# Infini-attention and a gated feed-forward layer: an order planned with margins, a second buffer for phi of Q, and a changed start

## The chip, the cores and the metric

The program runs on one core of one Trainium2 chip. The metric is the time of one execution on the device in microseconds. The kernel before took 832.03 us as the median of three runs (831.11 to 833.02).

Five engines work side by side: TensorE (PE; its weight loads are listed as PEld), VectorE (DVE), ScalarE (ACT), GpSimd (POOL), and SyncE (SP), which issues the DMAs. Each runs its own instructions strictly in the order in which the program lists them and waits on semaphores for the others.

## The reference

A layer with 2,048 tokens, width 512 and 32 heads of 16; the tokens fall in four segments of 512.

```python
x = A_x
h = x + attention(layernorm(x))        # N = 4 segments, H = 32 heads
h2 = h + geglu(layernorm(h))           # 512 -> 1376 -> 512

# attention, segment s, every head
logits = qs @ ks.T * scale + causal_mask
a_dot = softmax(logits) @ vs
pq = phi(qs)                           # phi(t) = t + 1 if t > 0 else exp(t)
a_mem = (pq @ M) / (pq @ z + 1e-6)     # memory of the earlier segments
o = sigmoid(beta) * a_mem + (1 - sigmoid(beta)) * a_dot
M, z = M + phi(ks).T @ vs, z + phi(ks).sum(0)

# feed-forward
out = (gelu(hn @ w_gate) * (hn @ w_up)) @ w_down
```

All data is float32. The kernel gets near that accuracy from TensorE's faster rounded format by splitting an operand into a high part (rounded) and a low part (the rest) and summing three products: high by high, high by low and low by high (`SPLIT`).

## The kernel before, in words

**Work.** The attention is cut into 16 units, one for each pair of a chunk of eight heads and a segment (`UNITS`, index `U`), and each unit into two halves of four heads (index `Q`, 0 to 31). Before them `ln1(s)` normalises the rows of segment `s`, transposes them on TensorE and splits them into `XT`. For each unit `qkv(U)` projects Q and K (`project`, L619), splits the result into `hl` (L680 on ScalarE, L682 on VectorE), sends it by DMA to the layouts `stq` and `stk`, computes phi of Q and K (`phi`: Relu L627 and Exp L629 on ScalarE, L631 on VectorE), and adds to the memory. `vproj` (L648) projects V for two units at a time.

Two passes over the scores follow for each half. `pass_a(Q)` computes scores with queries on the partitions (L797) and takes each row's extreme value on VectorE (L807, 512 instructions), which is moved into a free row of `stq`. `pass_b(Q)` computes the scores again with keys on the partitions (L862, L869), now with the extreme value subtracted by the matmul itself, takes the exponential on ScalarE (L876), masks the diagonal blocks on GpSimd (L879), and accumulates with V (L900) into one bank, `pv`. `mem(U)` reads phi of Q twice: for the denominator (L756) and, after a trip of the reciprocal through memory, for the numerator (L772).

`wo_seg` applies the output projection (L973); `ln2` normalises again; `ffn` computes gate and up products (L1145) and `down` the last product (L1206), with VectorE adding the result to the sum (L1211).

**Order.** No loop nest sets the order. Each piece of work is entered in a planner (`Sched`) as an operation of one engine with a planned duration, its operands and a due time. `Sched.run` walks through a planned time: among the operations that could start within a window of 0.059 us of the earliest one, it takes the one with the smallest due time, and emits it. So every engine's instruction order is fixed when the program is built. What shapes it:

- `DUE`: corrections to the due times, by kind of work (`q`, `k`, `d`, `v`, `m` by unit; `a`, `b`, `p`, `o` by half; `w`, `l` by segment), found by a search.
- `LAT`: the planned time from the end of an operation on one engine to a reader on another. `TAKEN`: the planned time until a buffer that it used is free.
- Pools (`Pool_`): buffers are taken when an operation starts and given back after the last user. The eight PSUM banks lie in `PD` (three, general: projections, transposes, memory), `PA` (two, scores of `pass_a`), `PB` (two, scores of `pass_b`) and `PPV` (one, the accumulation). A pool with `fifo=True` hands out buffers only in the order in which they were asked for. `acq` names buffers that an operation must obtain before it may start.

**The start.** For the first segment `layer_norm` runs 17 dummy transposes on TensorE while VectorE computes the scale (L497), then 16 transposes into four banks (L568, row block by row block, so that all four banks are complete only with the last row block). Each bank is split into `xt`: the high part by ScalarE (L588), the low part by VectorE (L589). Then Q and K of unit 0 are projected in two banks, chunk by chunk; the three products of a chunk are ordered high by high, weight's high by low part of `xt`, weight's low by high.

Of the kernel before, what the change touches and what calls it, by code (L numbers as in the profile page):

```python
# [15 lines left out]
P = 128  # L16
D = 512
T = 2048
NSEG = 4
NCH = 4  # L20
ND = D // P
# [12 lines left out]
DUE = {  # L34
# [85 lines left out]
class Op:  # L120
# [4 lines left out]

LAT = {
    "PE": {"PE": 0.0, "ACT": 0.27, "DVE": 0.246, "POOL": 0.24, "SP": 0.25},
    "ACT": {"PE": 0.14, "ACT": 0.12, "DVE": 0.137, "POOL": 0.172, "SP": 0.12},
    "DVE": {"PE": 0.108, "ACT": 0.12, "DVE": 0.17, "POOL": 0.165, "SP": 0.12},
    "POOL": {"PE": 0.085, "ACT": 0.08, "DVE": 0.09, "POOL": 0.12, "SP": 0.12},  # L130
}
TAKEN = {"PE": 0.22, "ACT": 0.14, "DVE": 0.12, "POOL": 0.1}
# [109 lines left out]
def infini_geglu(ctx: ExitStack, tc: tile.TileContext, x, wq, wk, wv, wo, beta,  # L242
# [29 lines left out]
    def dma(prio, fn, ins, outs, kb=256, dur=None, **k):  # L272
        return S.op("SP", dur or (0.4 if kb == 256 else 0.68), prio, fn, ins, outs, lat=kb / 290, **k)
# [40 lines left out]
    PPT = Pool_(many("pt", 2, [P, D]), then=PACC)  # L314
    PROW1 = Pool_(many("pt1", 9, [P, D]), then=PPT)
    PJ = Pool_(many("junk", 2, [P, D]), then=PC)
    PE_ = Pool_(many("e", 1, [P, D]), then=PC)
    PPQ = Pool_(many("pq", 1, [P, D]), then=PC)
# [32 lines left out]
    vh = Val(PJ)  # L351
# [104 lines left out]
    def layer_norm(prio, rows, dst, off=False, keep=None, acq=None, done=(), behind=(), scratch=None):  # L456
# [37 lines left out]
        if done and not behind:  # L494

            wm = Val(PB)
            pe(17 * 0.227, prio, lambda: [nc.tensor.transpose(  # L497
                wm.t[0:24, 0:P], bn.t.rearrange("p t k -> p (t k)"), ident) for n in range(17)],
                [bn, vident], [wm])
# [65 lines left out]
        if done and not behind:  # L565

            pts = [Val(PA if dc == 3 else PD) for dc in range(ND)]
# [56 lines left out]
    def phi(prio, pm, pool_):  # L624

        e, r = Val(PE_), Val(pool_)
# [38 lines left out]
    def qkv(U):  # L665
# [6 lines left out]
        for Q in half:  # L672
            STQ[Q], STK[Q] = Val(PSQ), Val(PSK)
        for i in range(2):
            hl = Val(PHL)
            if U == 0:
                HL0.append(hl)
            pm = project(first + 0.1 * i, W[s // 2, c, i], s, [hl])
# [6 lines left out]
            if i == 0 and s:  # L685
                PQ[U] = phi(first, pm, PPQ)
# [617 lines left out]
```

## Time and profile before

| | us |
|---|---|
| median of three runs | 832.03 (831.11 to 833.02) |
| the profiled execution, its time | 830.79 |
| its span, first to last instruction | 829.1 |
| TensorE busy | 805.0 |
| VectorE busy | 612.0 |
| ScalarE busy | 563.5 |
| GpSimd busy | 484.2 |

The granted TensorE clock was 1.00 throughout. How to read what follows: the page gives busy times, the chain that ended last and groups of instructions by line. In a row of waits, `PE bank L797 <- DVE nm L807` is TensorE's idle time before an instruction of line 797 that writes a bank, ended by VectorE's line 807. In a timeline row stand start, length, engine, line, operation, operands and number of merged instructions; in square brackets the engine's idle time before it and what ended it. Matmuls are pipelined: the row of one matmul of 512 columns lasts 0.39 us, while the next starts 0.23 us after it.

### The profile page before, as it was taken

What the parts mean: (1) busy time and instruction counts of PE and PEld (TensorE: products, weight loads), DVE (VectorE), ACT (ScalarE), POOL (GpSimd) and SP (SyncE); (2) the same over time, 40 slices, a digit from 0 to 9 for tenths busy, and PEclk for the clock granted to TensorE, in tenths of its full rate; (3) what the DMA queues carried; (4) which work ended last, traced back from release to release, by engine and by line L of the source; (5) the groups of instructions that cost most, each with busy time, mean ns of one, the idle gap of its engine ahead of it and who ended that gap; (6) DMA issues with size and microseconds to landing.
All of it is one profiled execution on the core that took longest, in us unless ns stands there. A gap on an engine that the chain in (4) does not pass through costs nothing.

```text
span 829.1 us, 15346 instructions
## 1 busy us (share of the span) xinstructions
PE 805.0 (97%) x4709; PEld 623.6 (75%) x4709; DVE 612.0 (74%) x1831; ACT 563.5 (68%) x1127; POOL 484.2 (58%) x719
## 2 busy tenths in 40 slices
PE   5999999999999999999999999999999999999998
PEld 4877767777777677776667677777888887788886
DVE  7888678788895878888896874676568856756565
ACT  6877868689988768776776862787467464545551
POOL 7533433444445444544736895788697686778750
PEclk9999999999999999999999999999999999999999
DMA  6543534565456564556554665531111341212102
GB/s 229 148 133 94 153 108 130 151 182 155 118 156 177 159 154 119 154 152 169 165 163 144 200 200 166 164 115 48 55 55 48 95 162 51 65 39 63 51 1 102
DMA packets 71750, 103.52 MB, mean 125 GB/s; under 512 B 14324, under 2 KB 24884, under 8 KB 71668
## 3 DMA queue, kind: packets, MB, share of 16 engines
q1 hardware_dynamic: 71668, 102.54, 42.6%
q8 instruction: 37, 0.61, 0.3%
q14 instruction: 45, 0.37, 0.2%
HBM read 54.92 MB, written 21.43 MB: 92 GB/s over the span
## 4 chain that ended last, share of the span: by engine, by line
PE 77%; DVE 10%; ACT 4%; issue 3%; POOL 3%; DMA 2%; SPq 1%; ACTq 0%; POOLq 0%; DVEq 0%
PE bank L1145 19%; PE bank L1206 14%; PE bank L619 8%; PE bank L797 8%; PE bank L869 7%; PE bank L900 7%; PE bank L973 4%; PE bank L648 4%; DVE junk L807 3%; ACT pt L876 1%; PE bank L726 1%; POOL raw L1122 1%; PE bank L772 1%; PE bank L579 1%; DVE hl L682 1%
## 5 line engine op out<-in xcount | busy, mean ns | idle before, releaser
L807 DVE CUSTOM_DVE_ANT_0 junk<-bank,amask 128x256 f32<-128x256 f32 (+3 forms) x512 | 228.3, 485 | 43.4 <-PE bank L797 40.3
L879 POOL TENSOR_SCALAR_AFFINE_SELECT pt<-pt 128x128 f32<-128x128 f32 (+2 forms) x352 | 118.8, 346 | 191.6 <-ACT pt L876 183.5
L876 ACT ACTIVATE pt<-bank 128x512 f32<-128x512 f32 (+1 forms) x352 | 181.4, 560 | 42.8 <-PE bank L869 36.4
L797 PE MATMUL bank<-stk,stq 128*128 128x512 f32 (+2 forms) x384 | 128.1, 377 | 4.3 <-DVE nm L807 3.9
L869 PE MATMUL bank<-stq,stk 128*128 128x384 f32 (+2 forms) x384 | 110.8, 351 | 1.7 <-ACT pt L876 1.4
L619 PE MATMUL bank<-xt,w 128*128 128x512 f32 x384 | 108.4, 394 | 1.1 <-DVE xt L589 1.1
L1211 DVE TENSOR_TENSOR pt<-pt,bank 128x512 f32<-128x512 f32 x96 | 65.0, 685 | 41.7 <-PE bank L1206 40.1
L797 PEld LDWEIGHTS bank<-stk,stq 128*128 128x128 f32 x384 | 68.6, 188 | 28.4 <-DVE nm L807 13.8
L869 PEld LDWEIGHTS bank<-stq,stk 128*128 128x128 f32 x384 | 67.3, 188 | 19.9 <-ACT pt L876 8.3
L619 PEld LDWEIGHTS bank<-xt,w 128*128 128x128 f32 x384 | 70.4, 188 | 12.5 <-DVE xt L589 1.3
L900 PE MATMUL bank<-pt,vaug 128*32 128x512 f32 (+3 forms) x1024 | 77.0, 436 | 0.0
L900 PEld LDWEIGHTS bank<-pt,vaug 128*32 128x32 f32 x1024 | 28.9, 109 | 39.1 <-issue 30.2
L648 PE MATMUL bank<-wv,xt 128*128 128x256 f32 x384 | 54.9, 283 | 0.0
L648 PEld LDWEIGHTS bank<-wv,xt 128*128 128x128 f32 x384 | 52.2, 189 | 1.8 <-issue 0.2
L1145 PE MATMUL bank<-xt,w 128*128 128x512 f32 (+1 forms) x186 | 51.2, 391 | 0.4 <-DVE n L1171 0.4
L1115 POOL TENSOR_TENSOR w<-raw,w 128x512 fp32r<-128x512 f32 (+3 forms) x37 | 42.0, 1137 | 6.8 <-ACT w L1113 6.6
L435 POOL TENSOR_TENSOR w<-raw,w 128x512 fp32r<-128x512 f32 (+1 forms) x23 | 29.7, 1291 | 22.3 <-ACT w L430 22.1
L807 DVE DVE_READ_ACCUMULATOR2_ANT nm<- 128x1 f32 x512 | 42.0, 82 | 0.0
L1145 PEld LDWEIGHTS bank<-xt,w 128*128 128x128 f32 (+1 forms) x186 | 34.3, 186 | 8.9 <-ACT ge L1163 0.8
L1145 PE MATMUL bank<-stk,w 128*128 128x512 f32 (+1 forms) x138 | 38.8, 390 | 0.0
L1122 POOL TENSOR_TENSOR raw<-raw,raw 128x256 f32<-128x256 f32 (+1 forms) x44 | 35.2, 799 | 2.9
L1122 POOL TENSOR_TENSOR raw<-raw 128x256 f32<-128x256 f32 (+1 forms) x44 | 33.6, 765 | 1.8
(298 smaller groups left out, 1798.5 us busy)
## 6 DMA issues: line engine op xcount, KB each, us to landing
stq<-hl SPq DMA_DIRECT2D x96, 128.0 KB
stk<-hl SPq DMA_DIRECT2D x192, 64.0 KB
pv_dram<-pvs SPq DMA_DIRECT2D x32, 256.0 KB
r<-r_dram SPq DMA_DIRECT2D x28, 256.0 KB
row<-x SPq DMA_DIRECT2D x24, 256.0 KB
raw<-wg SPq DMA_DIRECT2D x20, 256.0 KB
raw<-wu SPq DMA_DIRECT2D x20, 256.0 KB
raw<-wd SPq DMA_DIRECT2D x20, 256.0 KB
```

What stands on the lines that cost most here:

```text
L619: nc.tensor.matmul(pm.t, w.t[:, wi, dc * P:(dc + 1) * P], XT[s][dc].t[:, xi, :], start=dc == 0 and n == 0, stop=dc == ND - 1 and n == 2)
L648: nc.tensor.matmul(pm.t[:, 256 * t:256 * t + 256], XT[s][dc].t[:, xi, t0:t0 + P], whl[wi].t[:, h, 256 * (dc % 2):256 * (dc % 2) + 256], st ...
L797: nc.tensor.matmul(sa.t[:, k * w:(k + n) * w].rearrange("x (n w) -> x n w", n=n), sq.t[:, p, i * P:(i + 1) * P], sk.t[:, p, a:a + n, 0:w], ...
L807: nc.vector.tensor_tensor_reduce(out=junk.t[:, :w], in0=sa.t[:, k * w:(k + 1) * w], in1=amask[:, D - w:], op0=OP.add, op1=OP.min, scale=-1 ...
L869: nc.tensor.matmul(sc.t[:, lo:lo + D - q0], sk.t[:, p, a, q0:q0 + P], sq.t[:, p, q0:D], start=True, stop=True)
L876: act(w, prio, lambda: nc.scalar.activation(e.t[:, :w], sc.t[:, :w], AF.Exp), [sc], [e])
L879: nc.gpsimd.affine_select(v, v, pattern=pat + [[1, P]], compare_op=OP.is_ge, fill=0.0, base=0, channel_multiplier=-1)
L900: nc.tensor.matmul(pv.t[32 * n:32 * n + 32, kb * P:D], va.t[:, kb, 17 * j:17 * j + 32], e.t[:, lo:lo + D - kb * P], start=kb == 0, stop=la ...
L1122: pool(0.14 + 2.13e-3 * h, prio, lambda: nc.gpsimd.tensor_tensor(d.t[:, d0:d0 + h], a.t[:, a0:a0 + h], c.t[:, c0:c0 + h], op=o), ins, [d])
L1145: nc.tensor.matmul(dst.t[:w], v.t[:, wi, c0 + j * w:c0 + (j + 1) * w], b[bk][j].t[:, xi, :], start=first and j == 0 and n == 0, stop=j == ...
L1206: nc.tensor.matmul(pm.t, HH[p, f, s][hi].t[:w, t * P:(t + 1) * P], v.t[:w, wi, :], start=f == fl[0] and n == 0, stop=f == fl[-1] and n == 2)
L1211: dve(D, prio, lambda a=a, pm=pm: nc.vector.tensor_tensor(a.t, a.t, pm.t, op=OP.add), [pm], [a])
```

## The change

All parts come together in one step:

- **Margins.** The planned time from ScalarE, VectorE and GpSimd to TensorE grows by 0.4 us each; a buffer used by ScalarE or VectorE counts as free 0.1 us later. Some planned durations change (dummies, the accumulation with V, one kind of DMA issue). The `DUE` values are replaced by those of a new search.
- **Buffers.** `pq` has two buffers instead of one, `junk` one instead of two, so the memory used stays the same. `pass_a` writes the element-wise result of its reduction, which nobody reads, over the scores in the bank instead of into `junk`. The pool of exponentials `PPT` becomes first-in-first-out. The projection that feeds phi now obtains the buffer of phi's result before it starts; before, phi's first step obtained it.
- **Start.** 12 dummies instead of 17. The four transposed banks come from `PA`, `PA`, `PB` and `PD` instead of `PD` three times and `PA`. `project_two` projects Q and K of unit 0 together: for each chunk first the four matmuls that read only the high part of `xt` (two for Q, two for K), then the two that read the low part. The score passes keep their two banks each (`PA`, `PB`).

The diff, with the `DUE` values cut:

```diff
 LAT = {
     "PE": {"PE": 0.0, "ACT": 0.27, "DVE": 0.246, "POOL": 0.24, "SP": 0.25},
-    "ACT": {"PE": 0.14, "ACT": 0.12, "DVE": 0.137, "POOL": 0.172, "SP": 0.12},
-    "DVE": {"PE": 0.108, "ACT": 0.12, "DVE": 0.17, "POOL": 0.165, "SP": 0.12},
-    "POOL": {"PE": 0.085, "ACT": 0.08, "DVE": 0.09, "POOL": 0.12, "SP": 0.12},
+    "ACT": {"PE": 0.54, "ACT": 0.12, "DVE": 0.137, "POOL": 0.172, "SP": 0.12},
+    "DVE": {"PE": 0.508, "ACT": 0.12, "DVE": 0.17, "POOL": 0.165, "SP": 0.12},
+    "POOL": {"PE": 0.485, "ACT": 0.08, "DVE": 0.09, "POOL": 0.12, "SP": 0.12},
 }
-TAKEN = {"PE": 0.22, "ACT": 0.14, "DVE": 0.12, "POOL": 0.1}
+TAKEN = {"PE": 0.22, "ACT": 0.24, "DVE": 0.22, "POOL": 0.1}
...
-        return S.op("SP", dur or (0.4 if kb == 256 else 0.68), prio, fn, ins, outs, lat=kb / 290, **k)
+        return S.op("SP", dur or (0.4 if kb == 256 else 0.64), prio, fn, ins, outs, lat=kb / 290, **k)
...
-    PPT = Pool_(many("pt", 2, [P, D]), then=PACC)
+    PPT = Pool_(many("pt", 2, [P, D]), fifo=True, then=PACC)
...
-    PJ = Pool_(many("junk", 2, [P, D]), then=PC)
+    PJ = Pool_(many("junk", 1, [P, D]), then=PC)
...
-    PPQ = Pool_(many("pq", 1, [P, D]), then=PC)
+    PPQ = Pool_(many("pq", 2, [P, D]), then=PC)
...
-    vh = Val(PJ)
+    vh = Val(PE_)
...
-            pe(17 * 0.227, prio, lambda: [nc.tensor.transpose(
-                wm.t[0:24, 0:P], bn.t.rearrange("p t k -> p (t k)"), ident) for n in range(17)],
+            pe(12 * 0.21, prio, lambda: [nc.tensor.transpose(
+                wm.t[0:24, 0:P], bn.t.rearrange("p t k -> p (t k)"), ident) for n in range(12)],
...
-            pts = [Val(PA if dc == 3 else PD) for dc in range(ND)]
+            pts = [Val(pool_) for pool_ in ((PA, PA, PB, PD) if not behind else (PD, PD, PD, PA))]
...
+    def project_two(prio, w, s, acq):
+        pm = [Val(PD), Val(PD)]
+        for dc in range(ND):
+            def f(dc=dc):
+                for n, (i, wi, xi) in enumerate((i, wi, xi) for wis, xi in (((0, 1), 0), ((0,), 1))
+                                                for i in range(2) for wi in wis):
+                    nc.tensor.matmul(pm[i].t, w[i].t[:, wi, dc * P:(dc + 1) * P], XT[s][dc].t[:, xi, :],
+                                     start=dc == 0 and n in (0, 2), stop=dc == ND - 1 and n > 3)
+            pe(6 * mm(D), prio, f, [*w, XT[s][dc]], pm, acq=acq if dc == 0 else [])
+        return pm
+
-    def phi(prio, pm, pool_):
+    def phi(prio, pm, r):

-        e, r = Val(PE_), Val(pool_)
+        e = Val(PE_)
...
+        hls = Val(PHL), Val(PHL)
+        if U == 0:
+            first_two = project_two(first, [W[0, 0, 0], W[0, 0, 1]], 0, hls)
         for i in range(2):
-            hl = Val(PHL)
+            hl = hls[i]
             if U == 0:
                 HL0.append(hl)
-            pm = project(first + 0.1 * i, W[s // 2, c, i], s, [hl])
+            if i == 0 and s:
+                PQ[U] = Val(PPQ)
+            if i == 1 and s < NSEG - 1:
+                PQ[U, "k"] = Val(PPK)
+            r = PQ.get((U, (U, "k"))[i])
+            pm = project(first + 0.1 * i, W[s // 2, c, i], s, [hl] + ([r] if r else [])) if U else first_two[i]
...
-            if i == 0 and s:
-                PQ[U] = phi(first, pm, PPQ)
-            if i == 1 and s < NSEG - 1:
-                PQ[U, "k"] = phi(first, pm, PPK)
+            if r:
+                phi(first, pm, r)
...
-                junk = Val(PJ)
-
-                def g(k=k, a=a, p=p, junk=junk):
+                def g(k=k, a=a, p=p):
                     nc.vector.tensor_tensor_reduce(
-                        out=junk.t[:, :w], in0=sa.t[:, k * w:(k + 1) * w], in1=amask[:, D - w:],
+                        out=sa.t[:, k * w:(k + 1) * w], in0=sa.t[:, k * w:(k + 1) * w], in1=amask[:, D - w:],
                         op0=OP.add, op1=OP.min, scale=-1.0, scalar=BIG,
                         accum_out=nm.t[:, a, p, i:i + 1])
-                dve(w, prio, g, [sa, vamask], [junk, nm], chain=True)
+                dve(w, prio, g, [sa, vamask], [nm], chain=True)
...
-            pe(sum(0.02 + 0.86 * (4 - kb) / 4 for kb in kbs), Q + 1.122 + DUE["p"][Q], f,
+            pe(sum(0.735 * (4 - kb) / 4 for kb in kbs) + (0.17 if last else 0.06), Q + 1.122 + DUE["p"][Q], f,
```

34 rows, old and new, of the table DUE are left out of this document.

## The prediction

> **What bounds the kernel now.** I read the page first: busy shares and the chain of work that ended last.
>
> ```profile
> span 829.1 us, 15346 instructions
> PE 805.0 (97%) x4709; PEld 623.6 (75%) x4709; DVE 612.0 (74%) x1831; ACT 563.5 (68%) x1127; POOL 484.2 (58%) x719
> PE 77%; DVE 10%; ACT 4%; issue 3%; POOL 3%; DMA 2%; SPq 1%; ACTq 0%; POOLq 0%; DVEq 0%
> ```
>
> TensorE is busy for 97% of the span and carries 77% of the chain. No matmul is added or removed except five dummies, so the change can only win the time in which TensorE stands still or is held up. That is at most 24.1 us of visible idleness, and whatever hides inside "busy", because a matmul's row includes its pipeline. Where the idleness lies is told by sums over stretches (the attention, the feed-forward part, and two places looked at below):
>
> ```profile
> 44.00:470.00 426.00, 416.83 (x2943) 308.55 (x2943) 342.42 (x1334) 333.11 (x700) 201.97 (x426) 1.00 0.53 147
> 470.00:825.00 355.00, 353.55 (x1562) 286.38 (x1560) 232.17 (x378) 198.12 (x370) 256.32 (x245) 1.00 0.29 90
> 400.00:425.00 25.00, 22.99 (x161) 15.60 (x153) 22.79 (x85) 17.87 (x37) 14.87 (x29) 1.00 0.55 152
> 455.50:466.50 11.00, 9.38 (x74) 5.23 (x70) 7.80 (x21) 8.97 (x18) 7.60 (x15) 1.00 0.33 102
> ```
>
> The columns are length, then busy time of PE, PEld, DVE, ACT, POOL. TensorE idles 9.2 us in the attention stretch, 1.45 us in the feed-forward stretch; the rest, some 13 us, is the start and the last drain. Third, who made TensorE wait in the attention stretch, by its matmuls and by its weight loads:
>
> ```profile
> PE bank L797 <- DVE nm L807: 3.9, 8, 0.8
> PE bank L869 <- ACT pt L876: 1.4, 3, 0.5
> PE bank L830 <- DVE pk L631: 1.3, 1, 1.3
> ...
> PEld bank L900 <- issue: 30.2, 121, 0.4
> PEld bank L797 <- DVE nm L807: 13.6, 31, 1.7
> PEld bank L869 <- ACT pt L876: 8.3, 24, 1.0
> PEld bank L900 <- POOL pt L879: 7.0, 28, 0.4
> ```
>
> Columns: total, times, longest. The matmuls' own waits are few. The loads' waits on data (13.6 + 8.3 + 7.0 = 28.9 us, 83 times, 0.35 us on average) are partly hidden by the matmul still in the array. The reader is to see that these are mostly waits of a few tenths of a microsecond for VectorE's minimum, ScalarE's exponential or GpSimd's mask: operands placed to arrive just in time and arriving a little late. The 30.2 us ahead of L900's loads wait for nothing and are untouched by the change.
>
> **The change, part by part.**
>
> **1. Fewer dummies (17 to 12).** The first TensorE instructions and the rows that the transposes wait for:
>
> ```profile
> 7.61 3.58 PE L497 MATMUL bank<-ident,bn 128*24 128x128 f32 x17 [7.61 <-DVE bn L491]
> 11.02 1.91 PE L568 MATMUL bank<-ident,pt 128*128 128x128 f32 x16
> 14.02 5.75 PE L619 MATMUL bank<-xt,w 128*128 128x512 f32 x24 [1.08 <-DVE xt L589]
> 19.60 1.59 PE L648 MATMUL bank<-wv,xt 128*128 128x256 f32 x12
> ...
> 9.92 0.82 ACT L545 ACTIVATE pt<-pt,ln,ln 128x512 f32<-128x512 f32 x1 [0.52 <-DVE ln L539]
> 9.80 1.45 DVE L533 TENSOR_SCALAR pt<-pt,mv,ln 128x512 f32<-128x512 f32 x3
> ```
>
> Twelve dummies at 3.58/17 = 0.21 us end at about 10.1 instead of 11.0. The transposes go row by row, four for each; VectorE's three rows are ready at about 10.3, 10.8 and 11.25, ScalarE's at 10.74. The third row now binds: eight transposes of 0.12 from about 11.3 end at 12.2, where now all sixteen end at 12.93 with a last tail. I take 0.5 us.
>
> The dummies take 0.21 us apiece and the transposes 1.91/16 = 0.12, for the same 128 columns, so TensorE runs at about half rate until roughly 10.8, about 3.2 us after it began. After the change the transposes fill the place of the missing five dummies with a pause of some 0.2 us.
>
> The Trainium skill, TensorE: Matmul & The Clock Gate, section "What's actually happening", says that the array leaves half rate only after about one busy window of 3.4 us, which runs free of the kernel's start, so the moment wanders by half a microsecond; the trace agrees with about 3.2 us. By that rule twelve dummies (2.5 us) alone do not open the gate, and this speaks against the cut; if the pause voided the window, the whole would come to 829.0, the cold rival below, and if not, the sum of 826.0 stands.
>
> **2. First projections begin with high parts.** The chain there:
>
> ```profile
> 12.64 0.61 ACT xt L588
> 13.27 0.70 DVE xt L589
> 14.02 5.08 PE bank L619 x21
> 19.12 0.60 ACT hl L680
> ...
> 28.69 0.47 PE L797 MATMUL bank<-stk,stq 128*128 128x512 f32 x1
> ```
>
> The first of the 24 matmuls waits for VectorE's low part until 14.02. With four matmuls per chunk that read only the high part, it can go at ScalarE's end, 13.25: 0.7 us earlier. Four matmuls of 0.23 cover VectorE's 0.70 for the low part. The two gains add to 1.2 us for TensorE. But Q's bank was complete after 21 of 24 matmuls and is now complete after 23, two later (2 x 0.24 = 0.5 us), and the chain continues through that bank's copy at 19.12. What survives is 0.7 to 1.2; I take **-0.8 us**. The other end is 0, if something else (the next rows' normalisation on VectorE) sets the pace there. That the four transposed banks come from the score passes' pools costs nothing: the first score (L797, the last row) runs at 28.69, and it frees the two banks that both projections need together.
>
> **3. Margins of 0.4 us towards TensorE, and new due times.** This is planning alone: the order of instructions changes, none of them does. The margin exceeds the mean wait of 0.35 us above, though not the longest of 1.7, so most of these waits would have some projection or other filler placed in front. Visible idleness of 9.2 us is what surely can be won; 28.9 us is the ceiling if the waits hidden beneath matmuls are real throughput too. Nothing excludes a loss: filler used earlier is missing later (rival one). I take just over half of the visible idleness, **-5.0 us**, nearest to the matmuls' own row, because a wait of the loads that the running matmul covers is worth nothing. Ends: +8 and -14.5 (rivals).
> In the feed-forward stretch only the margin acts, on 1.45 us of idleness: **-0.4 us**, between 0 and -1.4. The altered planned costs (the accumulation with `vaug`, an SP issue at 0.64 for 0.68) are part of the same ordering. First-in-first-out exponential buffers constrain only the plan's order; I put them at nothing.
>
> **4. Two buffers for phi of Q.** Late in the attention each new value waits for the old one's last reader:
>
> ```profile
> 323.46 0.60 ACT L680 ACTIVATE hl<-bank 128x512 fp32r<-128x512 f32 x1
> 329.34 1.02 PE L772 MATMUL bank<-pq,mb 128*128 128x512 f32 x2
> 330.36 0.60 ACT L627 ACTIVATE e<-bank 128x512 f32<-128x512 f32 x1
> 332.01 0.69 DVE L631 SCALAR_TENSOR_TENSOR pq<-bank,e 128x512 f32<-128x512 f32 x1
> 354.58 1.02 PE L772 MATMUL bank<-pq,mb 128*128 128x512 f32 x2
> ```
>
> The projection was copied out at 323.46, but its bank stays held until 332.7, because `pq` is free only when L772 has read it at 330.3; the new value is then held until 355.6. That is a loop of about 25 us through one buffer, and one of the three general banks blocked for 9 us. A second buffer breaks it. None of TensorE's longest waits, quoted above, names it, so its worth is freedom for the planner and lies inside term 3. In return a projection now begins in the plan only when its phi buffer is free; `pk` stays single, which can delay a K projection. Without a row that shows it binding I put it at 0.
>
> **5. The minimum written in place.** The 512 reductions now write their unread result into PSUM, not into `junk`. Nearest pair of rows, the same addition to SBUF and to PSUM, and the group concerned:
>
> ```profile
> L1157 DVE TENSOR_TENSOR vaug<-vaug,bank x10: 682/687/689, 521.0 to 809.6; 128x512 f32<-128x512 f32 x9, 96x512 f32<-96x512 f32 x1
> L1157 DVE TENSOR_TENSOR bank<-vaug,bank x25: 680/696/697, 470.3 to 802.1; 128x512 f32<-128x512 f32 x22, 96x512 f32<-96x512 f32 x3
> ...
> L807 DVE CUSTOM_DVE_ANT_0 junk<-bank,amask 128x256 f32<-128x256 f32 (+3 forms) x512 | 228.3, 485 | 43.4 <-PE bank L797 40.3
> ```
>
> 9 ns x 512 = 4.6 us more VectorE work, over 342 busy of 426 us, so 84 us of idleness cover it. The minima differ by 2 ns the other way, so a gain of 1 us is not excluded. The cover is thin only where VectorE is full (22.79 of 25 us at 400 to 425). I take **+0.2 us**, ends -0.2 and +4.6.
>
> **Sum.** -0.8 - 5.0 - 0.4 + 0.2 = -6.0 us against the profiled execution, whose span is 829.1 and whose time is 830.79. That execution lies 1.2 below the median of the runs, 832.03; I put the difference on the median: **826.0 us**.
>
> **The rivals.**
> *Filler runs out (slower).* Projections and output products fill TensorE while scores wait. The last score pass has nearly none:
>
> ```profile
> 455.51 0.96 PE L973 MATMUL bank<-xt,wv 128*128 128x512 f32 x3
> 457.46 0.99 PE L869 MATMUL bank<-stq,stk 128*128 128x512 f32 x2 [0.52 <-ACT pt L876]
> 460.11 0.82 PE L869 MATMUL bank<-stq,stk 128*128 128x384 f32 x2 [0.47 <-ACT pt L876]
> 462.44 0.50 PE L869 MATMUL bank<-stq,stk 128*128 128x256 f32 x2 [0.37 <-ACT pt L876]
> 462.78 1.47 PE L579 MATMUL bank<-ident,row 128*128 128x128 f32 x12
> ```
>
> Its 11 us show 1.62 idle, and 0.96 + 1.47 of foreign work were laid into it: about 4.0 us lost per pass without filler. If the margins spend filler in the first units, each further bare pass costs 4.0. One still leaves a gain of 2; two decide it: 826.0 + 8 = 834; three give 838. For it: 400 to 425 already idles 2.0 us. Against it: the feed-forward products can begin before the last pass ends.
> *VectorE's load, not the order, makes the waits (no change).* At 400 to 425 VectorE is as full as TensorE (22.79 and 22.99); margins cannot make a full engine deliver. Then term 3 is 0: 832.03 - 1.0 = 831.0. Against it: over the whole stretch VectorE has 84 us to spare.
> *Hidden waits go too.* Half of 28.9 is 14.5 in place of 5.0: 816.5. For it: the loads' waits are longer in total than the matmuls'. Against: a load has the running matmul as its cover.
> *Cold start.* If the clock stays at half rate through 16 transposes (16 x 0.09 = 1.4) and 3.2 us of projections (half lost, 1.6), the start is worth 3.0 - 0.8 = +2.2 instead of -0.8: 829.0.
>
> **How the numbers follow.** Forecast (822 to 829) 0.42; hidden waits too 0.15; cold start 0.05; VectorE's load 0.15; filler runs out 0.23. A change of 0.2% (1.7 us) is about what a measurement of this kernel can tell from none: faster is below 830.4, slower above 833.7. VectorE's case lies at that edge and gives 0.05 to faster and 0.10 to same. So faster 0.67, same 0.10, slower 0.23. The range reaches from 816.5 down to 816 and up past two bare passes to 836; beyond it I leave some 0.07 below and 0.12 above. The likeliest case's own range is 822 to 829.
>
> **What would show it.** Right: the first projection at about 12.8 instead of 14.02, transposes still near 0.12 us apiece, TensorE's idleness from 44 to 470 near 4 us, the loads' wait for L807 well under 13.6, phi of Q no longer starting right behind L772, L807's mean at most 10 ns up. Wrong: bare score passes with waits for ScalarE at 350 to 470, a longer attention part, or projections of 0.4 us apiece at the start.

## The result: 12.1 us slower

The changed kernel takes 844.18 us (median of four runs, 842.79 to 846.48) against 832.08 for the kernel before beside it: 1.0148 times, 95% interval 1.0119 to 1.0177. The forecast was 826.0 with a range up to 836, so both sign and range missed. Its profiled execution took 842.98 us. The page after, first lines:

```profile
span 841.1 us, 15241 instructions
PE 814.6 (97%) x4704; PEld 626.0 (74%) x4704; DVE 631.9 (75%) x1831; ACT 564.5 (67%) x1127; POOL 484.1 (58%) x719
```

VectorE's busy time grew from 612.0 to 631.9 us with the same 1831 instructions. TensorE's grew as well, from 805.0 to 814.6 with five instructions fewer, so most of the 12 us do not show as idle time of TensorE: they lie inside rows that count as busy. The stretches of attention and feed-forward:

```profile
44.00:470.00 426.00, 414.82 (x2879) 302.74 (x2877) 355.95 (x1319) 327.56 (x684) 193.69 (x413) 1.00 0.52 143
470.00:825.00 355.00, 353.41 (x1580) 286.25 (x1580) 230.20 (x387) 204.51 (x386) 264.56 (x258) 0.99 0.29 91
```

Fewer instructions of every engine fit into the same 426 us (2879 matmul rows for 2943), and VectorE needs more time for fewer of them (355.95 us for 1319, where it was 342.42 for 1334). TensorE's idleness rose from 9.2 to 11.2 us. The waits in the attention stretch (total, times, longest):

```profile
PEld bank L816 <- DVE nm L824: 20.9, 55, 0.9
PEld bank L917 <- POOL pt L896: 4.7, 16, 0.4
PEld bank L886 <- ACT pt L893: 4.6, 13, 0.8
...
PE bank L816 <- DVE nm L824: 5.2, 14, 0.5
```

L816 and L824 are the old L797 and L807. The waits for VectorE's minimum grew from 13.6 to 20.9 us for the loads and from 3.9 to 5.2 for the matmuls. These are waits that the margins were to shorten. The other two that the prediction named fell: from 7.0 to 4.7 for GpSimd's mask and from 8.3 to 4.6 for ScalarE's exponential. What the reductions cost by shape, after (busy time, mean ns of one):

```profile
L824 DVE CUSTOM_DVE_ANT_0 bank<-bank,amask 128x512 f32<-128x512 f32 x128 | 87.5, 701 | 11.1 <-PE bank L816 11.0
L824 DVE DVE_READ_ACCUMULATOR2_ANT nm<- 128x1 f32 x512 | 71.6, 140 | 0.0
...
L824 DVE CUSTOM_DVE_ANT_0 bank<-bank,amask 128x128 f32<-128x128 f32 x128 | 38.8, 303 | 5.7 <-PE bank L816 2.4
```

and before:

```profile
L807 DVE CUSTOM_DVE_ANT_0 junk<-bank,amask 128x512 f32<-128x512 f32 x128 | 85.9, 683 | 13.1 <-PE bank L797 12.3
L807 DVE DVE_READ_ACCUMULATOR2_ANT nm<- 128x1 f32 x512 | 42.0, 82 | 0.0
L807 DVE CUSTOM_DVE_ANT_0 junk<-bank,amask 128x128 f32<-128x128 f32 x128 | 29.9, 286 | 4.2 <-PE bank L797 4.0
```

The reductions themselves are 17 and 18 ns longer in these two shapes, twice the 9 of the forecast. But each is followed by a read of the accumulated value, which the prediction had not looked at: 140 ns instead of 82. The timeline shows what the means hide. VectorE before, two of the four narrow reductions on one bank (start, length):

```profile
63.30 0.29 DVE L807 CUSTOM_DVE_ANT_0 junk<-bank,amask 128x128 f32<-128x128 f32 x1
63.51 0.08 DVE L807 DVE_READ_ACCUMULATOR2_ANT nm<- 128x1 f32 x1
63.51 0.29 DVE L807 CUSTOM_DVE_ANT_0 junk<-bank,amask 128x128 f32<-128x128 f32 x1
```

and after:

```profile
63.57 0.30 DVE L824 CUSTOM_DVE_ANT_0 bank<-bank,amask 128x128 f32<-128x128 f32 x1
63.79 0.14 DVE L824 DVE_READ_ACCUMULATOR2_ANT nm<- 128x1 f32 x1
63.96 0.30 DVE L824 CUSTOM_DVE_ANT_0 bank<-bank,amask 128x128 f32<-128x128 f32 x1
```

From start to start it is 0.39 us instead of 0.21. Before, the next reduction starts together with the read of the last one; now it starts 0.03 us after that read has ended. The instruction list of the two programs says why (VectorE, after, then before; each line has what is written, what is read and the engines waited for):

```
L824 bank_68,nm_148 <- bank_68,amask 128x128 [waits PE]
L824 bank_68,nm_148 <- bank_68,amask 128x128 [waits DVE]
L824 bank_68,nm_148 <- bank_68,amask 128x128 [waits DVE]
...
L807 junk_120,nm_148 <- bank_69,amask 128x128 [waits DVE,PE]
L807 junk_121,nm_148 <- bank_69,amask 128x128 [waits DVE]
```

In the changed kernel a reduction that follows another on the same bank waits for it, although it touches other columns: the earlier one now writes the bank, and the program tracks a bank as a whole. Before, the waits on VectorE itself were for the write two back, which had long ended. Narrow reductions come two to a bank (256 columns) or four (128), so each half has 2 + 3 = 5 such followers. At 0.18 us each (0.39 - 0.21 for 128 columns; 0.52 - 0.35 for 256 in the same timelines) that is 5 x 0.18 x 32 halves = 29 us of VectorE's time. The wide ones, of 384 and 512 columns, have a bank to themselves and no such wait.

### The profile page after: what moved, and what is told of

It reads as the page before. It is cut to its first block, busy times and chain, and to the rows that moved or that the text cites. A ratio compares the mean times of both kernels' runs of the same rounds, so it can differ in the third digit from the quotient of the medians.

```text
span 841.1 us, 15241 instructions
## 1 busy us (share of the span) xinstructions
PE 814.6 (97%) x4704; PEld 626.0 (74%) x4704; DVE 631.9 (75%) x1831; ACT 564.5 (67%) x1127; POOL 484.1 (58%) x719
## 4 chain that ended last, share of the span: by engine, by line
PE 47%; DVE 6%; ACT 2%; issue 1%; POOL 1%; DMA 0%; SPq 0%; DVEq 0%; ACTq 0%; POOLq 0%
PE bank L1162 24%; PE bank L1223 14%; PE bank L990 4%; DVE bank L824 2%; PE bank L917 1%; PE bank L816 1%; PE bank L886 1%; PE bank L580 1%; PE bank L620 1%; DVE nm L824 0%; DMA cd<-pv_dram 0%; ACT stk L1025 0%; ACT pt L893 0%; DVE bank L1019 0%; DVE row L994 0%
## 5 line engine op out<-in xcount | busy, mean ns | idle before, releaser
L824 DVE CUSTOM_DVE_ANT_0 bank<-bank,amask 128x256 f32<-128x256 f32 (+3 forms) x512 | 247.1, 504 | 47.0 <-PE bank L816 40.5
L816 PE MATMUL bank<-stk,stq 128*128 128x512 f32 (+2 forms) x384 | 134.3, 390 | 9.0 <-DVE nm L824 5.9
L886 PE MATMUL bank<-stq,stk 128*128 128x384 f32 (+2 forms) x384 | 114.2, 354 | 1.4 <-ACT pt L893 1.1
L620 PE MATMUL bank<-xt,w 128*128 128x512 f32 x360 | 102.7, 395 | 0.0
L816 PEld LDWEIGHTS bank<-stk,stq 128*128 128x128 f32 x384 | 68.5, 188 | 40.7 <-DVE nm L824 22.6
L620 PEld LDWEIGHTS bank<-xt,w 128*128 128x128 f32 x360 | 65.3, 188 | 9.9 <-DVE xt L590 0.2
L824 DVE DVE_READ_ACCUMULATOR2_ANT nm<- 128x1 f32 x512 | 71.6, 140 | 0.0
L436 POOL TENSOR_TENSOR w<-raw,w 128x512 fp32r<-128x512 f32 x25 | 32.3, 1294 | 30.6 <-ACT w L431 22.5
L1162 PE MATMUL bank<-xt,w 128*128 128x512 f32 (+1 forms) x168 | 47.0, 398 | 0.0
L1132 POOL TENSOR_TENSOR stk<-raw,stk 128x512 fp32r<-128x512 f32 (+3 forms) x28 | 31.1, 1113 | 23.0 <-PE bank L1162 14.5
L1162 PE MATMUL bank<-xt,stk 128*128 128x512 f32 (+1 forms) x138 | 38.1, 391 | 0.2 <-ACT pq L1169 0.2
```

The source lines that it names most:

```text
L620: nc.tensor.matmul(pm.t, w.t[:, wi, dc * P:(dc + 1) * P], XT[s][dc].t[:, xi, :], start=dc == 0 and n == 0, stop=dc == ND - 1 and n == 2)
L816: nc.tensor.matmul(sa.t[:, k * w:(k + n) * w].rearrange("x (n w) -> x n w", n=n), sq.t[:, p, i * P:(i + 1) * P], sk.t[:, p, a:a + n, 0:w], ...
L824: nc.vector.tensor_tensor_reduce(out=sa.t[:, k * w:(k + 1) * w], in0=sa.t[:, k * w:(k + 1) * w], in1=amask[:, D - w:], op0=OP.add, op1=OP. ...
L886: nc.tensor.matmul(sc.t[:, lo:lo + D - q0], sk.t[:, p, a, q0:q0 + P], sq.t[:, p, q0:D], start=True, stop=True)
L1132: pool(0.14 + 2.13e-3 * (hi - lo), prio, lambda: nc.gpsimd.tensor_tensor(v.t[:, 1, :hi - lo], r.t[:, lo:hi], v.t[:, 0, :hi - lo].bitcast(F ...
L1162: nc.tensor.matmul(dst.t[:w], v.t[:, wi, c0 + j * w:c0 + (j + 1) * w], b[bk][j].t[:, xi, :], start=first and j == 0 and n == 0, stop=j == ...
```

## The experiments

Theory A: these waits between neighbours on a bank are the loss. Rival B: the new order is. The kernel before, run again beside each group of experiments, took 831.72 to 832.37; every ratio below is to the one beside it.

**Without the narrow in-place writes (order untouched).** The 256- and 128-column reductions write slices of the single junk tile.

```diff
-  out=sa.t[:, k * w:(k + 1) * w],
+  out=(sa.t if w > 2 * P else junk_t[0])[:, k * w:(k + 1) * w],
```

> The changed kernel, instruction order untouched; only the reductions of 256 and 128 columns, of which two and four share a bank, write their unread result to SBUF (halves and quarters of junk) instead of into the bank; those of 512 and 384 columns stay in place. Theory A (written in place, a reduction waits for the one before it on the same bank: 392 instead of 211 ns from start to start at 128 columns, 524 instead of 345 at 256; 5 such followers in each half, 32 halves, 0.18 us each = 29 us of VectorE): the time falls by 10 to 16 us, to 828 to 834; the start to start falls to about 211 and 345 ns. Rival B (the new order is worse by itself): the time stays within 2 us of 844.

Measured 835.54: 1.0043 (1.0029 to 1.0056). From start to start on one bank it is 0.21 us again, so slices of this tile do not tie neighbours together as the bank did. Of the 12.1 us 8.6 go, less than the 10 to 16 that theory A expected, and 3.5 stay.

**All in place in the kernel before, order untouched.**

```diff
-  out=junk.t[:, :w],
+  out=sa.t[:, k * w:(k + 1) * w],
```

> The kernel before, instruction order untouched; only the reduction's unread result goes into the bank instead of junk. Theory A: slower than before by 10 to 16 us, 842 to 848; VectorE's start to start on one bank rises by about 0.18 us. Rival B: within 2 us of 832.

Measured 847.21: 1.0187 (1.0174 to 1.0200). This one part, by itself, costs the old order 15.5 us. It is enough for the loss.

**Wide ones and narrow ones apart, in the kernel before.**

```diff
+  out=sa.t[:, k * w:(k + 1) * w] if w > 2 * P else junk.t[:, :w],    # wide in place
...
+  out=sa.t[:, k * w:(k + 1) * w] if w <= 2 * P else junk.t[:, :w],   # narrow in place
```

> The kernel before, order untouched; only the reductions of 512 and 384 columns (one to a bank, 8 of the 16 in each half) write in place, the others write junk as before. If the whole cost in place is the wait between neighbours of one bank: within 2 us of 832. If the later read of the accumulator, which stands at 140 instead of 82 ns wherever the write goes to the bank, delays the bank's release to TensorE and counts too: 836 to 840 (15.6 of all in place, less the 8.6 that e1 gave back, is 7).

> The complement of e5: only the reductions of 256 and 128 columns write in place. Theory A (neighbours on one bank wait 0.18 us, 5 times a half, 29 us of VectorE in all): 839 to 843. If the cost lies in the wide ones instead: within 2 us of 832. If the two parts add: the excess of e5 and e6 together is about 15.6.

Wide alone 833.33: 1.0011 (1.0002 to 1.0020), about 1 us. Narrow alone 844.61: 1.0149 (1.0133 to 1.0164), 12.3 us, above the 839 to 843 that was expected. Together that is 13.2, 2.3 less than the 15.5 of both at once, so the two costs do not simply add; why is open. The wide ones pay the longer accumulator read as well, 58 ns each, and it costs next to nothing; the narrow ones pay the waits:

```profile
65.54 0.30 DVE L807 CUSTOM_DVE_ANT_0 bank<-bank,amask 128x128 f32<-128x128 f32 x1
65.76 0.14 DVE L807 DVE_READ_ACCUMULATOR2_ANT nm<- 128x1 f32 x1
65.94 0.30 DVE L807 CUSTOM_DVE_ANT_0 bank<-bank,amask 128x128 f32<-128x128 f32 x1
```

That is VectorE's timeline with the narrow ones in place: 0.40 from start to start again, in the old order.

**Fewer and shorter waits.** In the kernel before, only the last narrow reduction on each bank writes in place; it then waits only for the earlier ones' reads, three times per half.

```diff
+  out=sa.t[:, k * w:(k + 1) * w] if w <= 2 * P and k == len(heads) - 1 else junk.t[:, :w],
```

> A dose for theory A. The kernel before, order untouched; of the reductions of 256 and 128 columns only the last one on each bank writes in place, the others write junk. 3 instead of 5 reductions in each half then wait for their neighbour. If each such wait costs the same: 3/5 of the 12.3 us of e6, 832 + 7.4 = 839 to 840. If what costs is the write into the bank: also 6/16 to 3/8 of the narrow ones write there, 832 + 4.6 = 837. If it is the read of a bank that was just written: near 832.

Measured 836.36: 1.0044 (1.0027 to 1.0061), 3.7 to 4.0 us, half of what equal waits would cost. It lies near the 837 that was expected if the write into the bank were the cost itself; but that rival fails on the wide ones, which write into the bank 256 times for about 1 us, where these do so 96 times. The timeline shows that this wait is shorter:

```profile
65.64 0.29 DVE L807 CUSTOM_DVE_ANT_0 junk<-bank,amask 128x128 f32<-128x128 f32 x1
65.85 0.08 DVE L807 DVE_READ_ACCUMULATOR2_ANT nm<- 128x1 f32 x1
65.96 0.30 DVE L807 CUSTOM_DVE_ANT_0 bank<-bank,amask 128x128 f32<-128x128 f32 x1
```

0.32 instead of 0.21 from start to start, 0.11 to 0.12 more, not 0.18. Here as in the changed kernel the waiting reduction starts 0.03 us after the accumulator read ahead of it has ended. That read lasts 0.08 us here, because its own reduction wrote to `junk`, and 0.14 there; this is most of the difference. So 3 x 0.118 x 32 = 11.3 us of VectorE cost 3.7 to 4.0, and 28.8 us cost 12.3: 0.33 to 0.43 us of the total per microsecond. More wait costs more, somewhat beyond proportion.

**The remaining 3.5 us: first the wide ones.** As the first experiment, and the wide reductions write halves of the junk tile in bfloat16 that nobody reads.

> The changed kernel, order untouched, with no reduction in place: those of 256 and 128 columns write junk as in e1, those of 512 and 384 write two halves of junk in turn as bf16 (nobody reads them). If the wide ones cost too: 828 to 831, and the accumulator's read returns to about 82 ns. If not: 835, and the new order and start are 3.6 us worse by themselves.

Measured 835.37: 1.0040 (1.0025 to 1.0055). Nothing gained: the second outcome of the two. What it was to mean, that the new order and start are worse by themselves, did not hold. (VectorE waited 6.8 us for ScalarE's use of the same tile in it, which the last experiments explain.)

**The start undone.** As the first experiment, with 17 dummies and the old order of the first projections' matmuls, emitted at the same planned places.

```diff
-  for n in range(12)
+  for n in range(17)
...
-  for n, (i, wi, xi) in enumerate(... for wis, xi in (((0, 1), 0), ((0,), 1)) for i in range(2) for wi in wis):
+  for i in range(2):
+      for n, (wi, xi) in enumerate(SPLIT):
```

> e1 with the start of the kernel before inside the same planned order: 17 dummies are emitted in place of 12, and the first projections use their three products in the old order, low part of xt second. If the start's gain reaches the end: 0.7 to 1.2 us above e1 (835.5), 836.2 to 836.7. If it is lost on the way: within 0.4 us of e1. The first projection moves from 12.9 to about 14 us.

Measured 835.23: 1.0041 (1.0026 to 1.0056). The start's gain doesn't show at the end, within 1.6 us. The comparison is not clean: VectorE's waits for ScalarE's use of the junk tile, explained below, are 5.1 us here and 3.4 in the first experiment.

**A warm start in the kernel before.** 45 dummies that read only the identity and begin at 2.21 us.

```diff
-  wm.t[0:24, 0:P], bn.t.rearrange("p t k -> p (t k)"), ident) for n in range(17)]
+  wm.t[:, 0:P], ident, ident) for n in range(45)]
```

> The kernel before, order untouched; instead of 17 dummies that wait for VectorE's statistics until 7.6 us, 45 dummies that read only the identity, from about 2.3 us. The granted clock rose 3.1 to 5.9 us after the first dummy in the profiles so far; started at 2.3, it would be up by 8.2 at the latest, ahead of the transposes. If the start's cold clock reaches the end of the kernel: 0.5 to 1.5 us faster than before. If the start is absorbed later, as e8 suggests: within 0.4 us. If 45 are too many: slower by up to 1 us.

Measured 832.82: 1.0002 (0.9990 to 1.0015). The first projection began at 13.33 instead of 14.02, and nothing of it reached the end.

**Old due times in the changed code, without and with margins** (both with the first experiment's writes).

```diff
-DUE = { new search }
+DUE = { of the kernel before }      # both; the first also LAT and TAKEN of before
```

> The changed kernel's code (start, two buffers for phi of Q, first-in-first-out exponentials, planned durations), with the writes of e1, but the due times and the planned times to TensorE of the kernel before (margin 0, buffers free as before). If the start's gain of 1.1 us at the first projection survives and nothing else matters: 830 to 831. If the old due times do not fit the changed code: 834 to 840.

> As e3, with the margins of 0.4 us towards TensorE and the later release of buffers of the changed kernel, due times of the kernel before. If margins help by themselves: 3 to 6 us below e3. If margins spend filler too early: 2 to 8 us above e3. If they do nothing: within 1.5 us of e3.

Measured 847.28: 1.0185 (1.0169 to 1.0201), slower than either outcome expected, and 852.92: 1.0273 (1.0257 to 1.0289), slower again by 5.6 us with the margins. Due times found for one set of buffers and delays are worth little for another: the same values give 832 in their own kernel. This says nothing about margins at their own due times. Margins or new due times alone in the code of before were not tried: the planner finds no order for them there.

**Own searches with margins of 0, 0.2 and 0.4 us** (changed code, first experiment's writes; three searches of mine, of unequal length; the third only goes on from the changed kernel's due times).

> The changed kernel's code with the writes of e1, margin 0 (planned times to TensorE and releases as before), and due times of a search of my own with that margin; the planner's own end of this plan is 809.0, of the kernel before 810.0, of the changed kernel 812.8 (these count margins as if they were real). If a plan's length is what decides: 1 us below before to 2 us above. If plans without margin slip more on the chip: 3 to 8 us above e14's excess over its plan.

> As e12, margin 0.2 and later release, due times of a search with it; planned end 812.3. If margins reduce the slip against the plan by what they are: a time between e12's slip and e14's.

> As e12, margin 0.4 and later release, due times of the changed kernel searched a little further; planned end 812.7 (changed kernel 812.8). Expected as e1: 0.2 to 0.6% above before. If margins pay, e14 is faster than e12 though its plan is 3.7 us longer.

Measured 840.31, 837.55 and 835.82: 1.0102 (1.0085 to 1.0118), 1.0067 (1.0050 to 1.0084), 1.0046 (1.0030 to 1.0062). Each step of margin is faster, though the intervals of neighbouring steps meet or nearly meet. The planner's own ends, no measurement, are 809.0, 812.3 and 812.7: the planned order gets longer by 3.7 us, and the chip's excess over it falls from 31.3 to 23.1.

**The thin end of the attention.** The last score pass has little other work in it, and the granted clock (the third column from the right) fell there. After, 465 to 480:

```profile
465.00:480.00 15.00, 13.80 (x87) 8.74 (x83) 9.71 (x22) 10.06 (x19) 10.28 (x17) 0.77 0.36 106
```

Each score matmul of that pass is issued twice, with the same result, to keep TensorE occupied: in the first experiment's kernel, and in the kernel before with the warm start.

```diff
-  for p in range(2):
+  for p in [0, 1] * (1 + (Q == 31)):
...
-  for n, lo, _ in parts:
+  for n, lo, _ in parts * (1 + (Q == 31)):
```

> e1, order untouched, but in the last half's second score pass (the bare one) each score matmul is issued twice; the second overwrites the first with the same values. This adds 2.6 us of TensorE work where it waits for ScalarE's exponentials. In the profiles of the changed kernel and of e1 the granted clock stands at 0.5 for 6.83 us at just this place (471.5 to 478.4 and 464.0 to 470.8). If the thin use of TensorE there lets the clock fall, and this is what is left of the loss: the clock stays at 1.0 and the time falls by 1 to 3.4 us below e1, to 832 to 834.5. If the clock's fall costs nothing: up to 2.6 us above e1.

> The kernel before, order untouched, with the early dummies of e11 and each score matmul of the last half's second pass issued twice as in e10. In e11's profile the granted clock stood at 0.5 for 3.41 us at 463.3, in that pass. If that fall is what ate the earlier start: 0.5 to 2 us faster than before. If the last pass does not bound the kernel before: within 0.8 us of it.

Measured 834.75: 1.0025 (1.0011 to 1.0039), and 833.11: 1.0007 (0.9995 to 1.0019). The first may be 0.8 (by medians) to 1.5 us (by ratios) faster than without, but the intervals meet; the second gains nothing.

**The experiment's own wait.** So far the remainder pointed to the order. What ended the waits of VectorE and ScalarE in the first experiment says otherwise:

```profile
DVE junk L825 <- ACT junk L479: 2.5, 3, 0.8
...
ACT junk L479 <- DVE nm L825: 1.5, 2, 0.8
...
DVE junk L825 <- ACT junk L488: 0.9, 1, 0.9
...
ACT junk L488 <- DVE nm L825: 0.8, 2, 0.5
```

L479 and L488 are ScalarE's passes over the rows of the later normalisations; they too write the junk tile, of which there is now one. By moving the narrow writes there, I had made two engines wait for each other, 5.7 us in all, where neither does so in the changed kernel or in the one before. So I gave each a half of the tile, in bfloat16; the instructions' durations stayed the same (628 ns for L479, 630 with the shared tile).

```diff
-  junk.t, rows[t].t, AF.Copy, ...                       # AF.Square alike
+  junk.t.bitcast(bfloat16)[:, 0:D], rows[t].t, AF.Copy, ...
...
-  out=(sa.t if w > 2 * P else junk_t[0])[:, k * w:(k + 1) * w],
+  out=sa.t[:, k * w:(k + 1) * w] if w > 2 * P else junk_t[0].bitcast(bfloat16)[:, D + k * w:D + (k + 1) * w],
```

> In the changed kernel with the narrow reductions written to the junk tile, that tile is shared with ScalarE's two passes over each row of the later normalisations, and the reductions waited 3.4 us for it and ScalarE 2.3 us for the reductions. Here ScalarE writes the lower half of the tile in bfloat16 and the narrow reductions the upper half, so neither waits for the other; nothing else changes and no result depends on these elements. Theory A (what remains of the loss beside the in-place waits is the new order itself): as with the shared tile, 1.0043 times the kernel before, 1.0035 to 1.0055. Theory B (the sharing is part of the remainder): 3.4 us of VectorE's waits at the 0.33 to 0.43 us that the narrow in-place waits cost per microsecond give 1.1 to 1.5 us less, that is 1.0025 to 1.003.

Measured 830.88 (828.87 to 833.06) beside 832.18: 0.9981 (0.9969 to 0.9994). 4.7 us came back, three times what the theory of sharing expected: 0.8 us for each of the 5.7 us of these waits, where the waits on a bank cost 0.33 to 0.43. Why these weigh more is not shown. Nothing is left of the 3.5 us: with the same order and apart writes, the change is faster than the kernel before. Its attention stretch, and its waits there:

```profile
44.00:470.00 426.00, 419.89 (x2942) 311.00 (x2941) 345.00 (x1337) 334.04 (x699) 202.08 (x426) 0.99 0.53 147
470.00:825.00 355.00, 354.05 (x1566) 287.98 (x1565) 229.24 (x381) 197.89 (x373) 256.62 (x245) 1.00 0.30 91
```

```profile
PEld bank L817 <- DVE nm L825: 9.8, 27, 0.9
...
PEld bank L887 <- ACT pt L894: 6.5, 16, 0.9
PEld bank L918 <- POOL pt L897: 6.4, 22, 0.6
...
PE bank L817 <- DVE nm L825: 1.9, 5, 0.5
```

The waits for the minimum (L825) are now below those of before (9.8 for 13.6, 1.9 for 3.9), as the margins intend. Against the changed kernel, where they were 20.9 and 5.2, these two rows fall by 14.4 us and the median by 13.3.

**Apart writes and the thin end.** The same with the doubled matmuls of the last pass.

> The same, with each score matmul of the last half's second score pass issued twice, so that the array has no thin stretch there. If the clock's fall to half in that pass costs the end, this is 1 to 2 us faster than the run beside it, with a granted clock of 1.0 from 460 to 485; if not, the same within 1 us or slower by the doubled matmuls, some 30 of 0.2 to 0.3 us, at most 4 us where nothing covers them.

Measured 829.83: 0.9966 (0.9954 to 0.9978), the best kernel of the study. Without the doubling and with it, 460 to 465:

```profile
460.00:465.00 5.00, 4.83 (x19) 4.04 (x18) 2.90 (x7) 3.44 (x7) 4.28 (x6) 0.50 0.13 29
```

```profile
460.00:465.00 5.00, 4.43 (x24) 3.04 (x23) 4.30 (x13) 4.01 (x9) 3.37 (x10) 1.00 0.29 93
```

Here the clock stays up; the trace of this kernel has one fall elsewhere, of 3.41 us at 429.6. The time is 1.05 us less, but the intervals overlap; in both pairs of kernels of the changed order the sign was the same, in neither is it settled.

**No margins, apart writes.** The order searched without margins, with the tile's halves.

> The order searched without margins, of 1.0102 times the kernel before, now with ScalarE's and VectorE's unread results in halves of their own. In its shared form the reductions waited 1.7 us for ScalarE and ScalarE 1.1 us for them, half of the 5.7 us in the changed order, where taking the sharing away brought 4.5 us. Theory A (the margins pay): about 2 us go with the sharing and the order stays behind the changed one with apart writes (0.9981) by some 6 us: 1.007 to 1.009. Theory B (the sharing made the difference between margins): 0.998 to 1.001.

Measured 837.41: 1.0062 (1.0047 to 1.0076), 6.5 us slower than the changed order with apart writes. That is just below the 1.007 to 1.009 expected if the margins pay, and far above the 0.998 to 1.001 of the other theory. Beside that one's waits above:

```profile
PEld bank L811 <- DVE nm L819: 12.0, 30, 1.2
PEld bank L881 <- ACT pt L888: 11.6, 30, 0.9
PEld bank L912 <- POOL pt L891: 8.0, 28, 0.8
```

31.6 us of loads' waits for data instead of 22.7. The order with margins has the shorter ones; how much of this and of the 6.5 is the quality of the search can't be told from one search each.

## Why the prediction was wrong

**Step 5, the minimum written in place (+0.2, ends -0.2 and +4.6), failed**, and alone decides the sign. It priced the instruction alone, at 9 ns more where the runs show 17 and 18, and not the read behind it (58 ns more). Above all it left out what the write does to the neighbour: the wait on the same bank, 29 us of VectorE's time and 13.3 us of the total (changed kernel against apart writes; 12.3 in the old order). The upper end was no bound, because the row it rested on, an addition, is never followed by another on the same bank. That the step replaced a rotating pair of buffers by one shared operand stood in the diff, and a change that adds a wait calls for naming who queues behind it.

**The cover was no cover.** "84 us of idleness cover it" took an average for a cushion. The minimum lies on the way from one score bank to the next matmul that needs it; 0.33 to 0.46 us of each microsecond reached the end though VectorE idled for 70 us of the stretch (426 - 355.95). The rival "VectorE's load" had this thought, but with today's load, not with more.

**Step 3, margins and new order (-5.0), was too large.** With apart writes, TensorE idles 6.1 us in the attention stretch (forecast 4, before 9.2) and the loads wait 9.8 us for the minimum (before 13.6), so the waits fell as the step says; that the margins did it, and not the new due times or the buffers, is not shown. The whole change then gives -1.3 us in place of -6.0. Taking off the wide in-place writes, about +1, the rest of it gives some -2.3, an estimate that lets the parts add. Part of the reason may show in the planner's ends: margins lengthen the planned order itself (812.8 against 810.0 for the kernel before), a price that the term lacked. How much of it reaches the chip was not measured.

**The feed-forward term (-0.4)** fits: 0.95 us of idleness with apart writes for 1.45 before. In the changed kernel itself it was 1.59.

**Steps 1 and 2, the start (-0.8)**, were right at the place and not visible at the end. TensorE's start after:

```profile
7.65 2.72 PE L498 MATMUL bank<-ident,bn 128*24 128x128 f32 x12 [7.65 <-DVE bn L492]
10.44 2.08 PE L569 MATMUL bank<-ident,pt 128*128 128x128 f32 x16
12.88 5.75 PE L632 MATMUL bank<-xt,w 128*128 128x512 f32 x24 [0.36 <-ACT xt L589]
```

The first projection begins at 12.88 (forecast 12.8, before 14.02), released by ScalarE's high part. That is not so in every run: in the first experiment, with the same start, it began at 13.96, because the clock rose later (below). And with the old start put back, or a warm one added to the kernel before, the end didn't move, so the lower end named there, 0, was the better value.

**Step 4, two buffers for phi of Q**, did what it says. After, one value is written at 328.26 while the one before it is still to be read, at 337.30:

```profile
328.26 0.68 DVE L644 SCALAR_TENSOR_TENSOR pq<-bank,e 128x512 f32<-128x512 f32 x1
```

```profile
337.30 1.02 PE L791 MATMUL bank<-pq,mb 128*128 128x512 f32 x2
```

Its worth by itself was not measured.

**The rivals.** "Filler runs out" gave the slower side its 0.23 with times of 834 and 838, near the result for a reason that didn't hold: the thin last pass existed before, and keeping it full brings about 1 us at most. "Hidden waits go too" (816.5) did not come: even with apart writes the gain is 1.3 us. "VectorE's load" gave 831.0, near the 830.88 with apart writes, but with the waits unchanged, and they fell from 28.9 to 22.7 us for the loads. "Cold start" did not occur in the changed kernel's profile; it did in that of the best kernel (below), and cost it nothing that shows. None of the rivals named a wait between VectorE's own instructions.

## What to carry to other kernels

When a result that nobody reads is moved, look first at whom the new place makes wait: a whole bank may be tracked as one, and a slice of it then ties neighbours together that were free. (Slices and halves of the SBUF tile here were not tied.) Price an instruction from start to start in a run of them, with its accumulator read, not from its own mean. And read the waits of the experiment itself: here the first repair brought its own, and the remainder that looked like the fault of the new order was the experiment's.

## What the runs showed of the hardware

- A read of the accumulated value takes 82 ns when the reduction writes to SBUF, 140 when it writes to PSUM (111 on average where half do). Alone, it is hidden: the wide writes cost about 1 us.
- A reduction of VectorE that waits for the one ahead of it starts 0.03 us after that one's accumulator read has ended. From start to start this costs 0.18 us where the read takes 140 ns, and 0.12 where it takes 82.
- The granted clock rises at no fixed time. By the clock records of the traces it came up 3.07 us after the first dummy in the changed kernel, 3.23 in the kernel before, and between 2.75 and 5.98 us after TensorE's first instruction over all 20 profiles (a profile's clock column shows 1.00 even ahead of the first record). The changed kernel's 16 transposes, quoted above, took 2.08 us, 0.13 each. The best kernel of the study has the same instructions there:

```profile
7.45 2.71 PE L499 MATMUL bank<-ident,bn 128*24 128x128 f32 x12 [7.45 <-DVE bn L493]
10.24 3.39 PE L570 MATMUL bank<-ident,pt 128*128 128x128 f32 x16
13.97 5.73 PE L633 MATMUL bank<-xt,w 128*128 128x512 f32 x24 [0.33 <-ACT xt L590]
```

Its transposes took 0.21 us each, as the dummies at half rate do; the clock rose at 13.21, 5.76 us after the first dummy. The Trainium skill, TensorE: Matmul & The Clock Gate, section "What's actually happening", has the rise after a busy window of about 3.4 us, give or take half a microsecond; the measured spread is wider. And the first projection, 1.1 us later than in the changed kernel, did not keep this kernel from being the fastest.
- The clock can stand at half in a stretch where TensorE's rows show 4.83 busy of 5 us (460 to 465, above), and at full where they show 4.43. The busy share of the rows doesn't tell where it falls.
